# Routed attention and gated MLP on one core: the first two token tiles of the output layer also as a seven-product pair, with a rewritten order of work

## The chip, the cores and the metric

One Trainium2 chip, one of its cores. The metric is the device time of one execution in microseconds (us). The kernel before took 300.97 us (median of 3 runs, 300.54 to 301.33).

## What is computed

Four batches of eight heads attend over 768 tokens of 64 values. A query sees a key only if both are nearest to the same one of 16 centroids of their head. The heads' outputs side by side are the 512 features of 3072 tokens, which pass through a layer of 2048 gated units and an output layer.

```python
q_assign = argmax(einsum('bhsd,hcd->bhsc', q_n, c_n))      # k_assign likewise
mask = q_assign[:, :, :, None] == k_assign[:, :, None, :]
scores = where(mask, scale * q @ k.T, -1e9)
attn = exp(scores - max); attn = attn / (sum(attn) + 1e-9)
x = (attn @ v).transpose(0, 2, 1, 3).reshape(B * S, H * D)
h = x @ w_in;  g = h / (1 + exp(-h));  out = g @ w_out
```

## The kernel before

The order of all work is written by hand. `plan` (L722) is a list of short entries; the loop behind it reads them one after the other and `step` (L604) issues the instructions of each. Every engine runs its own instructions in the order of the list, and waits only for data and for buffers. An entry is an operation, a number, perhaps an engine (`A` ScalarE, `D` VectorE, `P` GpSimd) and perhaps a bank of PSUM (0 to 3). A bank is free again when its content has been read out. Two more pairs of banks hold scores.

The entries that the text below uses, with their functions:

- `r`, `hi`, `lo`, `ht`: load q and k of a head (SP's queue), split into a high and a low half-precision part, transpose by DMA into `ab` (SP's queue). `vl`, `v`: load and cast V.
- `L` or `l`, `ls`, `mx`, `ge`, `cm`, `ce`: routing. Logits on TensorE, sum, maximum and compare on VectorE, two transposes of the one-hot rows on TensorE (`cd_mm`, L216), their evacuation (`cd_ev`, L225, ScalarE or VectorE), which then goes by DMA into the rows of `ab` that add the mask to the scores.
- `qk` and `ex` (L315, L328): a unit is a head, a half of the queries and two key tiles: two score matmuls and one exponential. There are 192 units, and two score buffers, so qk of unit u+2 waits for ex of unit u. 48 units are a batch.
- `pv`, `nm`, `pt` or `xd`, `pe`: attention times V into a bank, normalisation on VectorE, transpose by TensorE or DMA into `xt`, evacuation.
- `e`, `t`, `g` (L388, L400, L404): four matmuls for a block of 128 hidden features and 384 tokens into a bank, tanh on ScalarE, gate on VectorE into `gt`; `e` 0 to 15 are the first half of batch 0, 16 to 31 the second.
- `b`, `bo` (L412, L419): a quarter of the plain output layer for one token tile, four matmuls of 512 columns; its evacuation on VectorE and store.
- `wc` (L434): combinations of quarters of `w_out` for the pairs, kept in `store`, or written over one quarter of it.
- `m`, `S`, `z`, `o` (class `Pair`, L445): the output layer for two token tiles by Strassen's scheme. Seven products of eight matmuls of 256 columns (`m`), four sums of gated tiles on VectorE (`S`), three intermediate evacuations on ScalarE (`z`), four outputs (`o`, one on ScalarE, three on VectorE). The number is ten times the pair's place in `duos` (L602) plus the step.
- `w`: weight loads through GpSimd's queue, each behind a small copy that reads the newest exponential's output; `w8` to `w11` are the four parts of `w_out`.

Before the change the tiles of a batch form the pairs (0, 1), (2, 5) and (3, 4), but in batch 0 tiles 0 and 1 are plain: `b0` to `b7`, `bo0`, `bo1`. The list puts them between units 42 and 48, where the first batch's second half is not yet gated.

Of the kernel before, what the change touches and what calls it, by code (L numbers as in the profile page):

```python
# [29 lines left out]
def kernel(  # L30
# [571 lines left out]
    duos = [Pair(b, x, y) for b in range(B) for x, y in ((0, 1), (2, 5), (3, 4)) if (b, x) != (0, 0)]  # L602

    def step(op, n, eng, banks):  # L604
# [133 lines left out]
        lo13 mx8 L10.2 ge8 cm8 mx10 ex44 b3 ex45 ce8.A wc1 ge10 bo0 pv6.1 nm6 qk46 l9.0 cm10 vl15 ht13 ls9 mx9 wc2 ge9
        qk47 hi12.A lo12 vl13 ht12 wc12 b4.3 ce10.A ex46 pt6.2 b5 cm9.0 ex47 hi14.A ce9.A pe6.A lo14 r16 pv7.1 nm7 b6
        L11.2 wc8 pt5.0 pe5.A pt7.1 pe7.A b7 mx11 ge11 cm11 v10.A v8.A ce11.A hi15.D qk48 e24.0 r17 ht14 bo1 lo15 ht15  # L740
        vl9 v11 vl14 vl16.P t24 g24 e21.3 t21 e18.2 qk49 g21 ex48 l13.1 ls13 mx13 e22.3 t18 g18 ex49 qk50 r18 l12.1
        ls12 mx12 v15.D ex50 e27.0 t27 g27 vl17 hi17.P t22 g22 hi16.P e20.2 t20 g20 qk51 e19.1 ge12 e16.0 qk52 e23.3
        ex51 qk53 t16 t19 g19 g16 ex52 t23 ex53 e29.2 t29 g23 cm12.1 ce12.D ge13 qk54 ex54 e26.0 g29 e30.3 t30 t26
        e25.1 t25 qk55 ex55 qk56 v13.D l15.2 g30 g26 ls15 g25 e17.3 t17 e28.0 lo16 od2 qk57 cm13.1 e31.2 g17 S3 ex56
        wc13 wc14 ce13.A qk58 r20 ht16 v9 pv8.3 nm8 ex57 qk59 ex58 qk60 t31 L14.1 ex59 ex60 m1.3 mx15 wc7 mx14 ge15
        g31 qk61 qk62 ge14 t28 g28 m7 wc15 S13 ex61 ex62 lo17 cm14 ce14.A wc9 hi18.P lo18 cm15.0 ce15.A m11.2 wc3 qk63
        qk64 v16 pv9.1 nm9 z0 v17 ht17 r19 S1 ex63 ex64 qk65 m2.0 vl21.P qk66 ex65 z10 S2 wc10 S4 S11 wc11 ex66 qk67
        ex67 m17 qk68 m6 pv10.1 ex68 z1 hi20.D qk69 ex69 qk70 ex70 m5 o0 qk71 ex71 l17.0 S12 m16 z2 nm10 z11 ls17
        hi19.D lo20 qk72 l16.1 qk73 ex72 ex73 ht18 l18.0 o3 ls18 mx17 od1 ge17 m15 qk74 qk75 ls16 mx18 mx16 lo19 m3
        ex74 qk76 m4 S14 xd9 xd8 ex75 qk77 z12 v14.A pv11.1 o13 ex76 r21 ge16 vl19 r22 hi22.P qk78 xd10 ht19 m14 nm11  # L750
        ex77 ex78 qk79 o1 ge18 pt11.1 o12 ex79 pe11.A m12.0 vl18.P o2 m13 qk80 o11 qk81 o10 pv12.0 ex80 qk82 ex81
        e34.2 v21.A nm12 ex82 qk83 ex83 e35.0 t35 lo22 qk84 e33.3 cs16 cs18 hi21.P cs17 r23 lo21 g35 pv13.1 qk85 t34
# [5 lines left out]
        e47.2 t47 g47 qk99 r25 m21.0 qk100 ex99 qk101 l22.1 ls22 mx22 m22.2 l23.3 z20 ex100 ex101 qk102 o20 ex102 ge22
        S21 ls23 qk103 pv16.2 cv19 ex103 qk104 e48.3 qk105 ex104 ex105 mx23 S22 m26 cs22 v22.D z21 t48 ge23 qk106
        qk107 ex106 ex107 nm16 S24 r24 cx21 v20 m25 z22 m27.1 cx22 cv20 qk108 v19 pv17.2 qk109 o23 hi24.D vl23.P cs23  # L760
        xd16 cx23 v23.D cv21 ex108 qk110 m23 cv22 ex109 g48 nm17 o21 m24 o22 ex110 qk111 lo24 ht24 e49.2 ex111 qk112
        e50.1 cv23 t49 vl25.P ex112 g49 qk113 xd17 e51.3 v24 t50 ex113 qk114 g50 e52.2 t51 pv18.0 ex114 g51 t52 e53.1
# [67 lines left out]
```

## Time and profile before

| what | us |
|---|---|
| median of the runs | 300.97 |
| the profiled execution | 301.45 |
| its span from first to last instruction | 299.7 |
| TensorE busy | 289.5 |
| ScalarE busy | 233.6 |
| VectorE busy | 222.1 |
| GpSimd busy | 72.6 |

In the lines of the profile PE is TensorE (PEld its weight loads), DVE VectorE, ACT ScalarE, POOL GpSimd, SP the engine that issues most DMAs. A line of a timeline gives the start, the time until the end, engine, line of the code, operation, output<-inputs, shapes and count, and in brackets how long the engine stood idle before it and what ended that. TensorE's matmuls overlap, so the time between two starts tells more than the time of one. A line of a stretch gives its ends, its length, and for PE, PEld, DVE, ACT and POOL the busy time with the number of instructions, then TensorE's granted clock, the DMA engines' share and GB/s. A line of a group gives count, total busy time and mean ns of one.

### The profile page before, as it was taken

To read this page: it belongs to the slowest core of one execution; us is meant where nothing else is said; L and a number is where in the kernel's file an instruction comes from. 1 tells how busy PE (TensorE), PEld (TensorE's weight loads), DVE (VectorE), ACT (ScalarE), POOL (GpSimd) and SP (SyncE) were. 2 spreads that over 40 slices of the span, in tenths; PEclk is the share of its full clock that TensorE was granted. 3 is DMA by queue.
4 is the path that set the end of the run, shared out by engine and by line. 5 is a ranking of instruction groups with operands and counts; after the bars stand their busy time and mean duration, and the time that the engine had idled before them with its cause. 6 is when DMAs were issued, how large, how long until landed. Compare 5 with 4: busy or idle time off the path is not lost.

```text
span 299.7 us, 8579 instructions
## 1 busy us (share of the span) xinstructions
PE 289.5 (97%) x3433; PEld 212.7 (71%) x3433; DVE 222.1 (74%) x482; ACT 233.6 (78%) x410; POOL 72.6 (24%) x125
## 2 busy tenths in 40 slices
PE   8899999999999999999989999999999999999994
PEld 3767666567568887667856887767867886776683
DVE  5898848789899895878657987788756733666763
ACT  5999899957888888998879876898669768965631
POOL 2655802000172027224354014220420000000000
PEclk9999999999999999999999999999999999999999
DMA  6999999999976979894598535968221102211103
GB/s 209 293 252 240 195 195 174 188 239 217 232 201 160 171 180 266 182 166 103 133 212 202 166 68 112 248 158 125 52 88 35 26 5 79 74 28 35 38 18 126
DMA packets 75368, 44.13 MB, mean 147 GB/s; under 512 B 54288, under 2 KB 71216, under 8 KB 75328
## 3 DMA queue, kind: packets, MB, share of 16 engines
q1 hardware_dynamic: 70560, 36.14, 51.2%
q0 software_dynamic: 4480, 7.15, 12.9%
q8 instruction: 27, 0.44, 0.7%
q10 hardware_dynamic: 288, 0.30, 0.3%
q14 instruction: 13, 0.11, 0.1%
HBM read 27.30 MB, written 6.29 MB: 112 GB/s over the span
## 4 chain that ended last, share of the span: by engine, by line
PE 74%; DMA 13%; ACT 4%; DVE 3%; issue 2%; SPq 1%; POOL 1%; ACTq 0%; DVEq 0%; POOLq 0%
PE ph L390 22%; PE xb L477 18%; PE pS L325 15%; PE pO L342 9%; DMA vn<-in_v_dram 6%; DMA ab<-hl 4%; PE yb L477 3%; PE psN L159 3%; ACT P L330 2%; PE po L417 2%; DMA ab<-cdt 1%; DMA ab<-cd 1%; DMA raw<-in_q_dram 1%; PE wb L477 1%; DVE hl L112 1%
## 5 line engine op out<-in xcount | busy, mean ns | idle before, releaser
L330 ACT ACTIVATE P<-pS 128x768 f16<-128x768 f32 x192 | 151.2, 816 | 21.6 <-PE pS L325 20.1
L390 PE MATMUL ph<-xt,win_s 128*128 128x384 f16 x512 | 96.4, 326 | 0.0
L405 DVE SCALAR_TENSOR_TENSOR gt<-tn,ph 128x384 f16<-128x384 f32 x128 | 68.0, 550 | 32.8 <-ACT tn L402 32.0
L325 PE MATMUL pS<-ab 128*128 128x384 f16 x384 | 87.1, 326 | 1.4 <-DMA ab<-cdt 0.8
L402 ACT ACTIVATE tn<-ph 128x384 f32<-128x384 f32 x128 | 60.8, 499 | 13.5 <-PE ph L390 10.2
L390 PEld LDWEIGHTS <-win_s 128*128 128x128 f16 x512 | 49.4, 98 | 30.8
L325 PEld LDWEIGHTS <-ab 128*128 128x128 f16 x384 | 34.3, 98 | 17.8 <-DMA ab<-cdt 1.1
L342 PEld LDWEIGHTS <-P 128*128 128x128 f16 x1152 | 39.8, 97 | 4.2 <-DVE cd L234 0.4
L342 PE MATMUL pO<-vt,P 128*128 128x65 f16 x1152 | 41.2, 193 | 0.0
L477 PEld LDWEIGHTS <-gt 128*128 128x128 f16 x352 | 33.9, 98 | 6.4 <-DVE xn L354 0.3
L112 DVE SCALAR_TENSOR_TENSOR hl<-raw,hl 128x768 f16<-128x768 f32 (+3 forms) x35 | 31.4, 901 | 0.6 <-ACT hl L103 0.3
L105 POOL TENSOR_SCALAR hl<-raw 128x768 f16<-128x768 f32 (+1 forms) x11 | 22.8, 2074 | 34.9 <-DMA raw<-in_k_dram 20.2
L477 PEld LDWEIGHTS <-s 128*128 128x128 f16 x264 | 25.5, 98 | 4.5
L159 PEld LDWEIGHTS <-ab 128*128 128x128 f16 x544 | 18.9, 97 | 6.3 <-DMA ab<-hl 2.1
L477 PE MATMUL xb<-wout_s,gt 128*128 128x256 f16 x176 | 22.7, 273 | 0.2 <-DVE xn L354 0.2
L499 ACT ACTIVATE ot<-xb 128x256 f32<-128x256 f32 x33 | 12.7, 386 | 12.3 <-PE xb L477 12.0
L159 PE MATMUL psN<-stk,ab 128*128 128x16 f16 (+1 forms) x544 | 20.1, 184 | 1.7 <-DMA ab<-hl 0.7
L477 PE MATMUL xb<-wc,s 128*128 128x256 f16 x160 | 20.7, 273 | 0.0
L354 DVE TENSOR_TENSOR xn<-pO,zr 128x384 f16<-128x384 f32 x32 | 17.8, 557 | 1.1
L199 POOL TENSOR_SCALAR od<-od 128x96 f16<-128x96 f16 x16 | 8.9, 559 | 39.3 <-DVE od L192 39.1
L212 POOL DMA_DIRECT2D ab<-cdt x16 | 8.8, 547 | 33.2 <-PE pS L325 11.9
L490 DVE TENSOR_TENSOR s<-gt 128x1024 f16<-128x1024 f16 x22 | 15.7, 715 | 1.3 <-PE xb L477 1.0
(93 smaller groups left out, 258.5 us busy)
## 6 DMA issues: line engine op xcount, KB each, us to landing
raw<-in_k_dram SPq DMA_DIRECT2D x31, 192.0 KB, 3.9
raw<-in_q_dram SPq DMA_DIRECT2D x24, 192.0 KB, 4.0
out_dram<-ot SPq DMA_DIRECT2D x18, 256.0 KB, 2.6
vn<-in_v_dram SPq DMA_DIRECT2D x21, 192.0 KB, 4.5
vn<-in_v_dram POOLq DMA_DIRECT2D x11, 192.0 KB, 3.6
win_s<-in_moe_w_in_dram POOLq DMA_DIRECT2D x8, 256.0 KB, 7.3
wout_s<-in_moe_w_out_dram POOLq DMA_DIRECT2D x4, 512.0 KB, 9.4
out_dram<-ot SPq DMA_DIRECT2D x12, 128.0 KB, 1.8
```

What stands on the lines that cost most here:

```text
L105: nc.gpsimd.tensor_scalar(out=o, in0=i, scalar1=QS, scalar2=None, op0=ALU.mult)
L112: nc.vector.scalar_tensor_tensor(out=hl[:, s, 1, :], in0=raws[job.name][:, s, :], scalar=QS, in1=hl[:, s, 0, :], op0=ALU.mult, op1=ALU.sub ...
L159: nc.tensor.matmul(L[:, n % 2, :, n // 2], ab[:, i, :], stk[:, job.groups[i // 3][0], x : x + w], start=(x == 0), stop=(x + w == 2 * HC),)
L325: nc.tensor.matmul(pS[:, e, 0:HALF], abs_[kj.name][:, kn, :], rhs, start=True, stop=True)
L330: nc.scalar.activation(out=P, in_=pst.pop(u)[:, :, 0:HALF], func=AF.Exp, bias=0.0, scale=ESC)
L342: nc.tensor.matmul(o[:, (2 * t + h) * VW : (2 * t + h + 1) * VW], Ps[i + h, c, j // 2][:, j % 2, ts(t, 128)], vtb[(i + h) % 13][:, j, 0:VW ...
L354: nc.vector.tensor_tensor(out=xn, in0=ov[:, :, 0:D], in1=zr.unsqueeze(2).to_broadcast([128, 2 * NM, D]), op=ALU.mult)
L390: nc.tensor.matmul(ph[:, 0:HALF], win_s[:, r, ts(fb, 128)], xts[b, c][:, r, :], start=(r == 0), stop=(r == NR - 1))
L402: nc.scalar.activation(out=tn, in_=phs[b, c, fb][:, 0:HALF], func=AF.Tanh, bias=0.0, scale=0.5)
L405: nc.vector.scalar_tensor_tensor(out=gt[:, fb, NM * c : NM * c + NM, :].rearrange("p t n -> p (t n)"), in0=tns.pop((b, c, fb)), scalar=1.0 ...
L477: nc.tensor.matmul(o, self.lhs(l, f), self.rhs(r, f), start=(f == 0 and opens), stop=(f == HB - 1), skip_group_check=True)
L490: nc.vector.tensor_tensor(out=o, in0=a, in1=b_, op=op)
```

## The change

The pair (0, 1) of batch 0 is made like the others, so `b` and `bo` are gone, and the list of entries is another from unit 30 to about unit 102 and from unit 119 to about unit 141; between and behind these only the numbers of the pairs differ, which are higher by one (`m21` was the first pair of batch 1, `m31` is). The diff, with the list cut to a few of its lines:

```diff
-    duos = [Pair(b, x, y) for b in range(B) for x, y in ((0, 1), (2, 5), (3, 4)) if (b, x) != (0, 0)]
+    duos = [Pair(b, x, y) for b in range(B) for x, y in ((0, 1), (2, 5), (3, 4))]
...
-        t7 ht11 wc6 r15 qk41 e9.0 g15 t12 ex41 qk42 t9 b0.3 qk43 g7 b1 ex42 wc0 qk44 g12 g9 hi13.D L8.1 ex43 b2 qk45
...
+        qk39 ex38 ex39 hi11.D e8.0 ht9 lo11 pe4.A t14 t8 qk40 e12.2 ex40 ht11 g14 L8.3 qk41 qk42 t12 g12 ex41 ex42 g8
+        mx8 ge8 e7.1 v11 qk43 e9.0 wc4 cm8 ce8.D v10 t7 g7 wc8 ex43 qk44 e10.1 qk45 t9 g9 wc1 hi13.A lo13 t10 S3 wc5
...
```

In the new list the 16 projections of the second half of batch 0 and the score units 42 to 58 come ahead of the products; the first product stands behind `e17` and `qk58`. `hi12` to `hi15`, `hi17` and `hi19` are on ScalarE, `hi16` and `hi18` on VectorE; of these the old list has `hi16`, `hi17` and `hi18` on GpSimd.

The first place is VectorE's queue around the routing of head 8, from the low part of another head (L112) ahead of it. The first `mxn` and `om` (`om_90`) are the maximum and the one-hot rows of head 8, `cd` its evacuated transposes, `gt` gates, `wc` combinations of output weights, `s` a sum of the pair. Before:

```order
L112 SCALAR_TENSOR_TENSOR hl<-raw,hl 128x12x64
L183 TENSOR_REDUCE mxn<-psN 128x12
L192 TENSOR_TENSOR om_90<-psN,mxn 128x192
L183 TENSOR_REDUCE mxn<-psN 128x12
L443 TENSOR_TENSOR wc<-wc,wout_s 128x512
L192 TENSOR_TENSOR om_91<-psN,mxn 128x192
L422 TENSOR_SCALAR ot<-po 128x512
```

and now:

```order
L112 SCALAR_TENSOR_TENSOR hl<-raw,hl 128x12x64
L405 SCALAR_TENSOR_TENSOR gt<-tn,ph 128x384 x3
L183 TENSOR_REDUCE mxn<-psN 128x12
L192 TENSOR_TENSOR om_90<-psN,mxn 128x192
L443 TENSOR_TENSOR wc<-wout_s 128x512
L234 TENSOR_SCALAR cd<-psN,kadd 96x256
L405 SCALAR_TENSOR_TENSOR gt<-tn,ph 128x384
L443 TENSOR_TENSOR wc<-wout_s 128x512
L405 SCALAR_TENSOR_TENSOR gt<-tn,ph 128x384
L443 TENSOR_TENSOR wc<-wc,wout_s 128x512
L112 SCALAR_TENSOR_TENSOR hl<-raw,hl 128x12x64
L490 TENSOR_TENSOR s_97<-gt 128x1024
```

The evacuation of head 8's transposes (`cd`) has come from ScalarE to VectorE, with gates `g7` and `g9`, weight combinations and the sum S3 behind it; the plain tile's output copy (`ot<-po`) is gone.

The second place is ScalarE's queue from exponential ex31 on (`P`; `tn` is a tanh, `xt` a copy of attention output, `cd` as above, `hl` the high part of a head). Before:

```order
L330 ACTIVATE P<-pS 128x768 x3
L402 ACTIVATE tn<-ph 128x384 x2
L330 ACTIVATE P<-pS 128x768
L402 ACTIVATE tn<-ph 128x384
L330 ACTIVATE P<-pS 128x768 x2
L402 ACTIVATE tn<-ph 128x384 x3
L330 ACTIVATE P<-pS 128x768
L402 ACTIVATE tn<-ph 128x384
L330 ACTIVATE P<-pS 128x768 x3
L402 ACTIVATE tn<-ph 128x384 x2
L330 ACTIVATE P<-pS 128x768
```

and now:

```order
L330 ACTIVATE P<-pS 128x768 x3
L402 ACTIVATE tn<-ph 128x384
L330 ACTIVATE P<-pS 128x768 x3
L402 ACTIVATE tn<-ph 128x384
L330 ACTIVATE P<-pS 128x768 x3
L372 ACTIVATE xt<-px 128x384
L402 ACTIVATE tn<-ph 128x384 x2
L330 ACTIVATE P<-pS 128x768
L402 ACTIVATE tn<-ph 128x384
L330 ACTIVATE P<-pS 128x768 x2
```

The old piece ends with ex41, the new one with ex41 and ex42; the new one has four tanh fewer in this piece (three fewer counted from ex28 on), and one copy `xt` more, which VectorE did before.

The third place is SP's queue behind the load of `vl10`; `raw` are loads of q and k, `vn` loads of V, `ab<-hl` the transposes by DMA. Before:

```order
L264 DMA vn<-in_v_dram 128x384
L92 DMA raw<-in_q_dram 128x384
L92 DMA raw<-in_k_dram 128x384
L264 DMA vn<-in_v_dram 128x384
L92 DMA raw<-in_q_dram 128x384
L92 DMA raw<-in_k_dram 128x384
L121 DMA_TRANSPOSE ab<-hl 128x12x128 x3
```

and now:

```order
L264 DMA vn<-in_v_dram 128x384
L121 DMA_TRANSPOSE ab<-hl 128x12x128
L92 DMA raw<-in_q_dram 128x384
L92 DMA raw<-in_k_dram 128x384
L92 DMA raw<-in_q_dram 128x384
L92 DMA raw<-in_k_dram 128x384
L264 DMA vn<-in_v_dram 128x384
L121 DMA_TRANSPOSE ab<-hl 128x12x128 x3
```

The transpose of head 8 goes out ahead of the loads instead of behind them.

More of the change, by code (lines that the diff above doesn't have):

```diff
@@ L738 @@
[L738 to L752, printed above, removed]
@@ L758 @@
[L758 to L762, printed above, removed]
@@ new lines @@
+        g46 qk96 ex96 qk97 t42 v21.D g47 g42 pv15.2 nm15 qk98 vl19.P ex97 ex98 mx21 vl24.P e43.1 t43 cv18 e45.3 t45
+        xd13 xd14 vl20 ge21 g43 g45 xd15 S33 qk99 cs21 m31.0 qk100 ex99 qk101 l22.1 ls22 mx22 m32.2 l23.3 z30 ex100
+        ex101 qk102 o30 ex102 ge22 S31 ls23 qk103 pv16.2 cv19 ex103 qk104 e48.3 qk105 ex104 ex105 mx23 S32 m36 cs22
+        v22.D z31 t48 ge23 qk106 qk107 ex106 ex107 nm16 S34 r24 cx21 v20 m35 z32 m37.1 cx22 cv20 qk108 v19 pv17.2
+        qk109 o33 hi24.D vl23.P cs23 xd16 cx23 v23.D cv21 ex108 qk110 m33 cv22 ex109 g48 nm17 o31 m34 o32 ex110 qk111
```

94 lines of the change are left out of this document (54 added, 40 removed).

## Prediction

> **What bounds the kernel now.** I read the first part of the page, then the same busy times cut into stretches, then TensorE's timeline row by row. The page:
>
> ```profile
> span 299.7 us, 8579 instructions
> PE 289.5 (97%) x3433; PEld 212.7 (71%) x3433; DVE 222.1 (74%) x482; ACT 233.6 (78%) x410; POOL 72.6 (24%) x125
> ```
>
> TensorE (PE) carries the span; no other engine comes near. But PE's ends are modelled, so I take its work from the distance between starts, which I call a step. The stretch in which the list of order differs most runs from the first pair of score matmuls that both lists place alike (qk30) to the point where the remaining order is alike again (qk102). PE's timeline there:
>
> ```profile
> 43.88 0.81 PE L325 MATMUL pS<-ab 128*128 128x384 f16 x4
> 44.53 1.26 PE L342 MATMUL pO<-vt,P 128*128 128x65 f16 x36
> 45.62 0.49 PE L325 MATMUL pS<-ab 128*128 128x384 f16 x2
> 45.95 0.81 PE L390 MATMUL ph<-xt,win_s 128*128 128x384 f16 x4
> 46.60 0.49 PE L325 MATMUL pS<-ab 128*128 128x384 f16 x2
> ...
> 56.96 1.03 PE L417 MATMUL po<-wout_s,gt 128*128 128x512 f16 x4
> 57.83 0.49 PE L325 MATMUL pS<-ab 128*128 128x384 f16 x2
> ...
> 60.25 0.77 PE L159 MATMUL psN<-stk,ab 128*128 128x16 f16 x24 [0.75 <-DMA ab<-hl]
> ...
> 62.05 0.76 PE L159 MATMUL psN<-stk,ab 128*128 128x16 f16 x24
> 62.66 0.29 PE L221 MATMUL psN<-ident,om 128*96 128x128 f16 x2
> 62.78 1.03 PE L417 MATMUL po<-wout_s,gt 128*128 128x512 f16 x4
> ...
> 139.28 0.51 PE L159 MATMUL psN<-stk,ab 128*128 128x32 f16 x12
> 139.63 0.81 PE L325 MATMUL pS<-ab 128*128 128x384 f16 x4
> ...
> 142.67 1.04 PE L477 MATMUL xb<-wc,s 128*128 128x256 f16 x8
> 143.54 0.81 PE L325 MATMUL pS<-ab 128*128 128x384 f16 x4
> ```
>
> qk30 starts at 43.88 and qk102 at 139.63, 95.75 us later. Steps: two score pairs 43.88 to 44.53, so 0.325 a pair; a `pv` of 36 matmuls 1.09; a projection `e` of four 0.65; a plain output quarter `b` of four 512-wide matmuls 0.87; a product `m` of eight 256-wide ones 0.87; routing logits 0.61 (`L`) or 0.35 (`l`); two one-hot transposes `cm` 0.12, and so 0.18 for the three of a `pt`. Between the two points the old list has 72 qk, 42 e, 12 pv, 16 m, 8 b, 4 L, 12 l, 8 cm, 5 pt: 23.4 + 27.3 + 13.1 + 13.9 + 7.0 + 2.4 + 4.2 + 1.0 + 0.9 = 93.2. So PE stands still for only 95.75 - 93.2 = **2.6 us** here, 0.75 of it in the row that waits for a transposed tile. That is all a better order could win.
>
> **The change, part by part.** *Arithmetic on PE.* Eight `b` (8 x 0.87 = 7.0) go, seven `m` (7 x 0.87 = 6.1) come: -0.87 us. Both are priced in this trace, as 4 x 512 and 8 x 256 columns with the same step, and all of it lies on PE.
>
> The Trainium skill ("TensorE: Matmul & The Clock Gate", Back-to-back issue gap) speaks against this saving: it gives a sustained pace of some 131 ns a matmul at 512 columns and 81 ns at 128, by which cutting the width saves little. By an estimate from that page, near 98 ns at 256, 32 x 0.131 = 4.2 us would go and 56 x 0.098 = 5.5 come, +1.3 us, and the time of the forecast below would be 304.3 us. The rows above disagree (0.87 for four of 512 and for eight of 256).
>
> *Arithmetic elsewhere.* On DVE four sums of 0.61 and three output adds come and two output copies go; on ACT four evacuations come. Stores keep their number and bytes. Beside what they lie:
>
> ```profile
> 84.40:139.63 55.23, 54.52 (x726) 41.87 (x725) 45.98 (x98) 48.59 (x83) 18.26 (x28) 1.00 0.84 177
> 162.30:193.00 30.70, 30.70 (x374) 24.24 (x373) 24.49 (x51) 23.83 (x42) 6.79 (x13) 1.00 0.61 151
> ```
>
> After 84.4 DVE is busy 45.98 of 55.23 us and ACT 48.59, so these additions find room there; without it they would cost at most some 2.5 us of DVE. They are counted below where they fall earlier. The second re-ordered stretch lies in the second row: PE has no gap, DVE and ACT are 80% busy, and the list holds the same PE instructions. I take 0 and keep +-0.4.
>
> *Order in the first stretch.* This decides. The new list runs the attention ahead and leaves output products for later: between qk30 and qk48 PE had 27.0 us of the steps above and now has 19.2. ACT and DVE have hardly less than before, so they pace PE there. On SP the transpose of head 8 is moved past two pairs of loads and a V load, on POOL three casts leave for ACT and DVE. What comes later by that is first read on ACT behind ex43, so I cost it at nothing; where that cover fails is the second rival. Four terms give when PE reaches the first product m1, which in the new list opens the bank that the gate g28 on DVE frees.
>
> (1) ACT up to exponential ex41:
>
> ```profile
> 42.07 0.82 ACT L330 ACTIVATE P<-pS 128x768 f16<-128x768 f32 x1
> ...
> 49.72 1.53 ACT L330 ACTIVATE P<-pS 128x768 f16<-128x768 f32 x2
> 51.12 1.28 ACT L402 ACTIVATE tn<-ph 128x384 f32<-128x384 f32 x3
> 52.23 0.88 ACT L330 ACTIVATE P<-pS 128x768 f16<-128x768 f32 x1
> ...
> 56.66 0.83 ACT L330 ACTIVATE P<-pS 128x768 f16<-128x768 f32 x1
> ```
>
> and, from the groups by line, the copy of transposed tiles that the new list puts on ACT here:
>
> ```profile
> L372 ACT ACTIVATE xt<-px 128x384 f16<-128x384 f16 x4 | 1.9, 488 | 1.7 <-PE px L363 1.7
> ```
>
> Steps: exponential 0.70 (two from 49.72 to 51.12), tanh 0.37 (three to 52.23). The old list does 13 exponentials and 13 tanh from ex28 (42.07) to the start of ex41 (56.66): 13.9 of 14.6 us, so it loses 0.7. The new one does 14, 10 and one 0.49 copy to the end of ex41: 14.0, with the same loss 56.7.
>
> (2) qk43 needs ex41's buffer. Behind it PE does one `e` and then cm8: 56.7 + 0.33 + 0.65 + the 0.29 of row 62.66 = 58.0. The evacuation of cm8 now stands on DVE:
>
> ```profile
> L234 DVE TENSOR_SCALAR cd<-psC,kadd 96x256 f16<-96x256 f32 x1 | 0.5, 473 | 0.0
> ```
>
> With 0.4 of its 0.47, DVE is free for the gate g7 at 58.4. This is the added wait; all of DVE's queue stands behind it, and PE's next `e` waits for g7's bank.
>
> (3) From g7 to g28 DVE has 55 operations. Their steps, from rows that follow each other closely:
>
> ```profile
> 41.84 1.02 DVE L405 SCALAR_TENSOR_TENSOR gt<-tn,ph 128x384 f16<-128x384 f32 x2 [1.79 <-ACT tn L402]
> ...
> 65.65 0.55 DVE L168 TENSOR_REDUCE L<-psN 128x192 f32<-128x384 f32 x1
> 66.23 0.49 DVE L183 TENSOR_REDUCE mxn<-L 128x12 f32<-128x192 f32 x1
> 66.64 0.41 DVE L443 TENSOR_TENSOR wc<-wout_s,wc 128x512 f16<-128x512 f16 x1
> 66.98 0.35 DVE L192 TENSOR_TENSOR om<-L,mxn 128x192 f16<-128x192 f32 x1
> 67.25 0.95 DVE L112 SCALAR_TENSOR_TENSOR hl<-raw,hl 128x768 f16<-128x768 f32 x1
> 68.11 0.42 DVE L443 TENSOR_TENSOR wc<-wout_s 128x512 f16<-128x512 f16 x1
> ...
> 69.32 0.19 DVE L352 RECIPROCAL zr<-pO 128x6 f32<-128x6 f32 x1
> ...
> 70.02 0.41 DVE L443 TENSOR_TENSOR wc<-wout_s 128x512 f16<-128x512 f16 x1
> ...
> 98.07 0.69 DVE L490 TENSOR_TENSOR s<-gt 128x1024 f16<-128x1024 f16 x1
> 98.68 0.42 DVE L443 TENSOR_TENSOR wc<-wout_s,wc 128x512 f16<-128x512 f16 x1
> ```
>
> Gate 0.46 (1.02 less the 0.56 of one); logit sum 0.58; maximum 0.41; weight combination 0.34; compare 0.27; low part `lo` 0.86; normalisation 0.70; Strassen sum 0.61. 18 x 0.46 + 11 x 0.34 + 5 x 0.86 + 2 x 0.61 + 6 x 0.41 + 6 x 0.27 + 2 x 0.70 + 4 x 0.58 + one cast at most 0.86 = 26.2. So m1 starts near 58.4 + 26.2 = **84.6**. PE's own steps from qk30 to m1 are 36.1 and would allow 80.0, so PE stands 4.6 us.
>
> (4) From m1 to qk102 PE has 23 m, 43 qk, 16 e, 8 pv, 8 l, a cm and a pt: 56.2 us. DVE and ACT have less than that here (the row 84.40:139.63), so I add no wait. qk102 starts at 84.6 + 56.2 = 140.8 against 139.63: **+1.2 us**, that is -0.9 of work and +2.0 of standing. From there on the PE order is that of before.
>
> The profiled execution took 301.45 us, 1.75 around its span of 299.7; that is 0.5 above the median of 300.97. Added to the median: **302.1 us**. Bounds of the unknown: term 1's loss between 0 and twice 0.7; term 3 between 24.9 (a twentieth less) and 27.5 (waits for tanh as in the row above, in part). So m1 lies between 82.6 and 86.6, and the time between 300.1 and 304.1; half of that to each side is this case's own range, 301.1 to 303.1.
>
> **Rivals.**
>
> *DVE is quicker, and the order wins.* In the stretch 44 to 95 POOL casts 128x768 tiles beside DVE, and the sums are slow there:
>
> ```profile
> L490 DVE TENSOR_TENSOR s<-gt 128x1024 f16<-128x1024 f16 x2 | 1.9, 962 | 0.0
> ```
>
> 962 ns, against 0.69 us in the row at 98.07. The new list moves three such casts off POOL, and if POOL is what slows DVE, all 55 operations gain. At 10% less, 23.6, and without ACT's loss, m1 comes at 81.3 and qk102 at 137.5, 298.8 us; at half of both, 83.0 and 139.2, 300.5; I put it between, at 299.6. It decides for faster from the point where DVE's stretch is under 24 us, that is m1 before 82.5. Against it: the steps I used are from moments without such a cast too.
>
> *DVE waits for weights.* Behind g7 stands a weight combination that needs the last quarter of `wout_s`:
>
> ```profile
> 46.39 0.75 POOL L529 DMA_DIRECT2D wout_s<-in_moe_w_out_dram  x1 [0.53 <-issue]
> DMA to landing us min/median/max: 6.9/9.4/11.1
> ```
>
> Issued at 46.39 it lands at 57.5 with the longest of these; DVE comes to it at 58.9 and the margin is 1.4 us. In the new order a transpose and a load of SP's queue go out ahead of it, on the same DMA engines. If it comes 2.5 us later, DVE stands 1.1, m1 moves as much, 303.2 us.
>
> *The change does not do what it says*: seven narrower products, with 56 weight loads for 32, take PE as long as eight plain quarters. Then the 0.87 is not saved, 303.0 us. For it speaks only that each product is one more switch of operand; the equal steps at 56.96 and 142.67 speak against it.
>
> **How the numbers follow.** A measurement of this kernel can tell 0.3%, 0.9 us, from no change: 300.1 to 301.9. Forecast 0.53: as 302.1 is just beyond the upper border and its range reaches below it, 0.33 slower and 0.20 same. Quicker DVE 0.28: 0.25 faster, 0.03 same. Late weights 0.17 and dear products 0.02: slower. So faster 0.25, same 0.23, slower 0.52. The range runs from 299.1, half-way into the first rival, to 303.9, past the second: some 0.1 is left out at either end.
>
> **What would show it.** Right: PE's row reaches the first `xb` at 84 to 85; in the rows of 50 to 85 PE has many idle entries after DVE's gates and ACT's exponentials in place of the one after the DMA; DVE's cast L234 on `psN` starts near 58 and DVE is over 90% busy from there to 84; `xb` keeps a step of 0.87 for eight; from m1 to the score pair of unit 102 it takes 56 us. Wrong: `xb` before 82.5 (DVE or ACT quicker than their old steps), DVE idle behind a DMA of `wout_s`, or a loss after 141, where I count none.

## The result, and the profile after

| | before | after |
|---|---|---|
| median of 20 runs each, us | 300.30 | 301.86 |
| lowest and highest | 298.35, 302.07 | 300.70, 304.75 |
| the profiled execution | 301.45 | 301.82 |
| its span | 299.7 | 300.0 |

The ratio is 1.0061, with a 95% interval of 1.0040 to 1.0082: the change makes the kernel slower by 0.6%, 1.6 us between the medians. The forecast was 302.1.

The first lines of the changed kernel's page say as little as before. PE is busy for all but 10 us:

```profile
span 300.0 us, 8619 instructions
PE 289.6 (97%) x3457; PEld 215.3 (72%) x3457; DVE 222.3 (74%) x488; ACT 235.3 (78%) x413; POOL 67.1 (22%) x121
```

PE's timeline tells it, with the same points as in the prediction. 44.55 is qk30, 60.24 is e10 behind the gate g7, 68.08 is qk48, 85.42 is the first product m1, and 141.81 is qk102:

```profile
44.55 0.81 PE L325 MATMUL pS<-ab 128*128 128x384 f16 x4
45.67 0.81 PE L390 MATMUL ph<-xt,win_s 128*128 128x384 f16 x4 [0.31 <-DVE gt L405]
...
50.99 0.48 PE L325 MATMUL pS<-ab 128*128 128x384 f16 x2 [0.22 <-ACT P L330]
...
55.32 0.81 PE L390 MATMUL ph<-xt,win_s 128*128 128x384 f16 x4 [0.30 <-ACT xt L372]
...
58.93 0.28 PE L221 MATMUL psN<-ident,om 128*96 128x128 f16 x2
...
60.24 0.81 PE L390 MATMUL ph<-xt,win_s 128*128 128x384 f16 x4 [0.71 <-DVE gt L405]
...
65.55 0.96 PE L342 MATMUL pO<-vt,P 128*128 128x65 f16 x26 [0.41 <-ACT P L330]
...
67.91 0.34 PE L363 MATMUL px<-ident,xn 128*128 128x128 f16 x3 [0.53 <-DVE xn L354]
68.08 0.49 PE L325 MATMUL pS<-ab 128*128 128x384 f16 x2
...
74.96 1.46 PE L390 MATMUL ph<-xt,win_s 128*128 128x384 f16 x8 [0.23 <-DVE L L168]
...
85.42 1.04 PE L477 MATMUL xb<-wout_s,gt 128*128 128x256 f16 x8
...
141.81 0.81 PE L325 MATMUL pS<-ab 128*128 128x384 f16 x4
```

The reader is to see many small waits, behind ACT and DVE in turn, where the old list had, up to qk48, one of 0.75 us behind a transpose. The same stretch as sums, from g7 to m1, from m1 to qk102, and units 119 to 141:

```profile
59.64:85.42 25.78, 23.88 (x313) 16.68 (x313) 25.54 (x59) 23.61 (x45) 1.75 (x3) 1.00 1.04 198
85.42:141.81 56.39, 56.39 (x727) 44.50 (x725) 44.85 (x96) 45.89 (x79) 12.75 (x23) 1.00 0.81 179
163.50:194.20 30.70, 30.70 (x374) 24.25 (x373) 24.09 (x50) 23.82 (x42) 8.03 (x13) 1.00 0.69 153
```

DVE is busy for 25.54 of 25.78 us ahead of m1, ACT for 23.61. Behind m1 PE has no gap, and in the second reordered stretch it has as little as before.

**The account.** I call *stand* what is left when the steps of the prediction are taken from the distance between two of PE's starts; it holds the time that PE waits, and also the time that it loses by working more slowly than those steps. The two traces give:

| stretch | before: distance, steps, stand | after | after less before |
|---|---|---|---|
| qk30 to qk102 | 95.75, 93.17, 2.58 | 97.26, 92.33, 4.93 | +1.51 |
| qk102 to qk118 | 20.33, 19.33, 1.00 | 19.35, 19.33, 0.01 | -0.98 |
| qk118 to qk191 | 104.02, 103.96, 0.06 | 104.02, 103.96, 0.06 | 0.00 |

So the change lost 1.51 us where the list was rewritten, -0.84 of work and +2.35 of standing, and 0.98 came back just behind it. There the kernel before waited ahead of qk111 for a head's transposed one-hot rows, which a DMA puts into `ab`. Its chain and its PE rows:

```profile
146.69 4.00 DMA ab<-cdt
```

```profile
148.89 1.04 PE L477 MATMUL wb<-wc,gt 128*128 128x256 f16 x8
...
150.73 0.50 PE L325 MATMUL pS<-ab 128*128 128x384 f16 x2 [0.81 <-DMA ab<-cdt]
```

and the same place after, where qk111 follows its product at once:

```profile
151.07 1.04 PE L477 MATMUL wb<-wc,gt 128*128 128x256 f16 x8
151.94 0.49 PE L325 MATMUL pS<-ab 128*128 128x384 f16 x2
```

In these two executions, then, the change cost +0.53 us. Beside it qk30 came 0.67 us later, although the list ahead of it differs only in its last entries (`e2`, `t2` and `ht8` where `t1` and `e5` stood); in the twelve traces of the new list it starts anywhere from 43.06 to 44.82. And the last store landed 0.9 sooner behind the last matmul: from the start of the last product to the end it is 4.96 and 4.88 us in the two traces of the old list (the second is of an experiment below) and 4.04 to 4.45 in all twelve of the new one, a gain that the prediction did not have and whose cause the traces do not show. The medians differ by 1.56. The profiled execution of before was one of its longer ones, 1.15 above its median, that of after lies at its median; the remaining 1.0 us has no place in this pair of traces. The other trace of the old list lies 0.85 above its median and has a stand of a microsecond behind qk102 too. An execution of the old list without that stand would be shorter by about as much, and the loss would then be the 1.51 of the first row; that this is the usual execution is not shown.

### The profile page after: what moved, and what is told of

The parts are those of the page before. It is cut to its first block, busy times and chain, and to the rows that moved or that the text cites. A ratio compares the mean times of both kernels' runs of the same rounds, so it can differ in the third digit from the quotient of the medians.

```text
span 300.0 us, 8619 instructions
## 1 busy us (share of the span) xinstructions
PE 289.6 (97%) x3457; PEld 215.3 (72%) x3457; DVE 222.3 (74%) x488; ACT 235.3 (78%) x413; POOL 67.1 (22%) x121
## 4 chain that ended last, share of the span: by engine, by line
PE 79%; DMA 7%; DVE 5%; ACT 5%; issue 2%; POOL 1%; SPq 0%; ACTq 0%; POOLq 0%
PE ph L390 24%; PE xb L477 20%; PE pS L325 17%; PE pO L342 9%; DMA vn<-in_v_dram 5%; PE yb L477 3%; PE psN L159 3%; ACT P L330 2%; DMA raw<-in_q_dram 1%; DMA ab<-cd 1%; PE wb L477 1%; DVE hl L112 1%; DVE gt L405 1%; ACT hl L103 1%; ACT ab L144 1%
## 5 line engine op out<-in xcount | busy, mean ns | idle before, releaser
L402 ACT ACTIVATE tn<-ph 128x384 f32<-128x384 f32 x128 | 61.6, 500 | 12.5 <-PE ph L390 9.6
L477 PEld LDWEIGHTS <-gt 128*128 128x128 f16 x384 | 37.1, 98 | 7.2
L112 DVE SCALAR_TENSOR_TENSOR hl<-raw,hl 128x768 f16<-128x768 f32 (+3 forms) x35 | 31.9, 913 | 0.7 <-ACT hl L103 0.5
L477 PEld LDWEIGHTS <-s 128*128 128x128 f16 x288 | 27.9, 98 | 5.1
L272 POOL CAST vt<-vn 128x384 f16<-128x384 f32 x19 | 12.4, 661 | 55.1 <-DMA vn<-in_v_dram 55.1
L477 PE MATMUL xb<-wout_s,gt 128*128 128x256 f16 x192 | 24.6, 273 | 0.0
L499 ACT ACTIVATE ot<-xb 128x256 f32<-128x256 f32 x36 | 13.8, 384 | 11.5 <-PE xb L477 11.1
L477 PE MATMUL xb<-wc,s 128*128 128x256 f16 x176 | 22.8, 273 | 0.0
L105 POOL TENSOR_SCALAR hl<-raw 128x768 f16<-128x768 f32 (+1 forms) x8 | 16.3, 2034 | 12.9 <-ACT P L330 7.0
L508 DVE SCALAR_TENSOR_TENSOR ot<-xb,ot 128x256 f32<-128x256 f32 x20 | 8.5, 423 | 13.8 <-ACT ot L499 5.5
```

Of the source, the lines that this page charges most:

```text
L105: nc.gpsimd.tensor_scalar(out=o, in0=i, scalar1=QS, scalar2=None, op0=ALU.mult)
L112: nc.vector.scalar_tensor_tensor(out=hl[:, s, 1, :], in0=raws[job.name][:, s, :], scalar=QS, in1=hl[:, s, 0, :], op0=ALU.mult, op1=ALU.sub ...
L402: nc.scalar.activation(out=tn, in_=phs[b, c, fb][:, 0:HALF], func=AF.Tanh, bias=0.0, scale=0.5)
L477: nc.tensor.matmul(o, self.lhs(l, f), self.rhs(r, f), start=(f == 0 and opens), stop=(f == HB - 1), skip_group_check=True)
L499: nc.scalar.activation(out=o, in_=self.xb[:, 0:DH], func=AF.Copy, bias=0.0, scale=0.5)
```

## The experiments

Each kernel was timed beside the kernel before on the same chip. The stands are worked out from each kernel's one profiled execution, as above. It was the shortest of the kernel's runs in e1_dve_order, e2_wc_on_pool and e4_gate_first, and the longest in e5_norms_first, e8_more_dve and e13_head13_early. The experiments go by these full names, or in short as run e1, run e2 and so on; `e10` or `e12` without the word run are projections, as in the list.

| kernel | ratio to before | 95% | PE's stand qk30 to e12, to e10, to qk48, to m1, m1 to qk102 | qk30 to m1 |
|---|---|---|---|---|
| changed kernel | 1.0061 | 1.0040 to 1.0082 | 1.59, 0.93, 1.79, 0.50, 0.12 | 40.88 |
| e1_dve_order | 1.0278 | 1.0245 to 1.0312 | 1.59, 0.93, 1.27, 1.79, 6.14 | 41.65 |
| e2_wc_on_pool | 1.0111 | 1.0082 to 1.0141 | 1.59, 0.93, 1.57, 2.18, 0.11 | 42.34 |
| e3_plain_in_new_order | 1.0109 | 1.0074 to 1.0145 | 6.32 in all to the first quarter | 42.39 |
| e4_gate_first | 1.0033 | 1.0003 to 1.0063 | 1.59, 0.38, 2.17, 0.59, 0.11 | 40.80 |
| e5_norms_first | 1.0073 | 1.0039 to 1.0108 | 1.59, 1.90, 4.06, 1.17, 0.11 | 44.78 |
| e7_four_moves | 1.0055 | 1.0024 to 1.0087 | 1.12, 0.47, 1.36, 3.04, 0.11 | 42.05 |
| e8_more_dve | 1.0113 | 1.0067 to 1.0159 | 1.59, 0.93, 1.78, 2.59, 0.11 | 42.96 |
| e9_weights_wait_less | 1.0079 | 1.0049 to 1.0109 | 1.59, 0.93, 1.47, 1.31, 0.11 | 41.36 |
| e10_less_in_the_way | 1.0085 | 1.0050 to 1.0121 | 1.12, 0.47, 4.21, 1.41, 0.12 | 43.27 |
| e12_after_late_load | 1.0074 | 1.0050 to 1.0099 | 1.59, 0.94, 1.79, 1.23, 0.11 | 41.60 |
| e13_head13_early | 1.0055 | 1.0035 to 1.0075 | 1.12, 3.19, 2.30, 1.40, 0.11 | 44.08 |
| e11_before_early_load (before's list) | 1.0017 | 0.9988 to 1.0046 | | |

In runs e5, e10 and e13 not all of the stand is waiting: some 1.5 to 1.7 us of it is work at half the granted clock, as shown below for run e5.

The theory at the start was the prediction's: DVE's queue from g7 to g28 paces PE up to m1. Rivals: some other engine, or the landings of DMAs, hold m1 as well.

### Less work on DVE ahead of m1

Eleven operations are taken from DVE's queue ahead of g28 and done behind it; the orders of PE and ACT stay. (`hi16` and `hi18` come later too, with their low parts and transposes.)

```diff
-... S3 wc5 wc2 ... wc9 ... wc6 ... wc3 ... S1 ... wc13 ... wc7 ... wc10 ... hi18.D ... g28 ...
+... S3 ... g28 ... g17 S1 wc1 wc5 wc9 wc13 S2 ... wc3 wc7 wc11 wc15 ... S4 ... wc14 wc2 wc6 wc10 hi18.D lo18 ht18
```

> Same instructions as the changed kernel, and the same order on PE and ACT; on DVE nine weight combinations (9 x 0.34), the sum S1 (0.60) and one cast (0.46) stand behind the gate g28 instead of ahead of it, so that DVE has 4.1 us less between g7 and g28. Theory (DVE's queue paces PE up to the first product): the first product starts 2 to 2.6 us earlier than the 85.4 of the changed kernel, at 82.8 to 83.4, because PE's own steps from cm8 (58.9) take 23.3 us and become the limit; the time falls by about 2 us to 299.8, ratio to the kernel before 0.998. Rival A (ACT, or the round trip through four banks, paces): the first product stays at 85.4, ratio 1.006. Rival B (DVE only owes the work): the first product is earlier, but PE stands for the sums behind it and the time falls by less than 0.5 us.

The stretch from g7 to m1, to be read against the row 59.64:85.42:

```profile
58.15:84.70 26.55, 24.07 (x313) 16.37 (x313) 22.36 (x47) 23.67 (x45) 1.92 (x3) 1.00 1.02 212
```

DVE has 47 operations here instead of 59 and is busy 3.2 us less, but the stretch takes 26.55 us instead of 25.78. PE's rows say what took DVE's place, and what the moved work does later:

```profile
69.05 0.52 PE L159 MATMUL psN<-stk,ab 128*128 128x32 f16 x12 [1.23 <-DMA ab<-hl]
...
95.78 1.03 PE L477 MATMUL xb<-wout_s,gt 128*128 128x256 f16 x8 [1.09 <-DVE cd L234]
...
102.29 1.03 PE L477 MATMUL xb<-wout_s,s 128*128 128x256 f16 x8 [3.61 <-DVE ot L508]
```

The logits of head 13 (l13, at 69.05) wait for its transpose by DMA, a wait that the changed kernel's trace does not have. With what comes of it in PE's starts it is 1.40 us; by an estimate from these rows, m1 would without it have come 40.25 us behind qk30, 0.6 sooner than in the changed kernel, for 3.2 us less of DVE. And between m1 and qk102, where the prediction found room on DVE, PE stands 6.14 us instead of 0.12. The room is not where the work came to stand; just behind m1 the changed kernel's DVE has none, 9.73 of 10.00:

```profile
85.00:95.00 10.00, 10.00 (x139) 8.50 (x138) 9.73 (x22) 8.39 (x15) 1.78 (x3) 1.00 0.85 165
```

That DVE alone paces is refuted; m1 was to come 2 to 2.6 us earlier.

### The same work on GpSimd

```diff
-... t7 g7 wc8 ... wc1 ... wc5 wc2 ... wc9 ... wc6 ... wc3 ... wc12 ... wc13 ... wc7 ... wc10 ...
+... t7 g7 wc8.P ... wc1.P ... wc5.P wc2.P ... wc9.P ... wc6.P ... wc3.P ... wc12.P ... wc13.P ... wc7.P ... wc10.P ...
```

> The changed kernel with the eleven weight combinations between g7 and g28 on POOL, which is idle there, so DVE loses 11 x 0.34 = 3.7 us. Theory (DVE's queue paces, and POOL does not hurt it): first product at 82.5 to 83.4, time down by about 2 us, ratio 0.998 to the kernel before. Rival (POOL and DVE hinder each other, as the 962 ns sums beside POOL casts suggested): each DVE operation beside a combination is longer, the first product comes at 85 or later, ratio 1.006 or more.

Ratio 1.0111, as the rival had it. DVE and POOL side by side:

```profile
59.89 1.28 DVE L112 SCALAR_TENSOR_TENSOR hl<-raw,hl 128x768 f16<-128x768 f32 x1 [0.17 <-ACT hl L103]
61.10 1.64 DVE L490 TENSOR_TENSOR s<-gt 128x1024 f16<-128x1024 f16 x1
62.15 1.61 POOL L443 TENSOR_TENSOR wc<-wout_s,wc 128x512 f16<-128x512 f16 x1
62.66 0.54 DVE L405 SCALAR_TENSOR_TENSOR gt<-tn,ph 128x384 f16<-128x384 f32 x1
```

A combination that takes DVE 0.42 takes POOL 1.15 to 1.9 us, and beside it DVE's sum takes 1.64 instead of the 0.68 it has in the changed kernel and `lo` 1.28 instead of 0.95, while the gate, which reads PSUM, keeps its 0.54. The Trainium skill ("SBUF — State Buffer", SBUF: two separate sides) says that a GpSimd operation that reads SBUF and a VectorE operation with two SBUF inputs lock each other out for a whole instruction; the extra 0.96 us of the sum and 0.33 of `lo`, each less than the 1.15 of the shortest POOL operation, can be such waits, though no row shows the lock itself. So the first rival's mechanism exists. But taking three casts off GpSimd did not bring its gain: that rival needed DVE's stretch under 24 us, and the changed kernel's is 25.78. And l13 waits for its DMA here too, 0.54 us.

### The plain tiles in the new order

Tiles 0 and 1 plain again, at the places of the pair's products; the sums, `z` and `o` of the pair go, and four combinations that overwrite `wout_s` come behind the last quarter.

```diff
-... m1.1 qk59 m7 ... S2 ... z0 m6 ... S4 ... m2.2 ... z1 ... m5 ... z2 o3 ... m3 ... o0 m4 ... o1 ... o2 ...
+... b0.1 b1 qk59 b2 ... b3 bo0 ... b4.2 ... b5 ... b6 ... b7 bo1 wc3 wc7 wc11 wc15 ...
```

> The new order with tiles 0 and 1 plain again: eight quarters at the places of the seven products, the four sums of that pair gone, the in-place weight combinations behind the last quarter. It takes the pair alone away. PE gets 0.87 us more work; DVE gets two sums (1.2) and two combinations (0.7) less between g7 and g28. Theory (DVE paces): the first quarter starts 1.9 us earlier than the first product did, at 83.5, and the whole is about 1 us shorter than the changed kernel, ratio to the kernel before 1.002 to 1.004: the pair costs more than it saves in this order. Rival A (the pair simply saves its PE work): 0.9 us longer than the changed kernel, ratio 1.009. Rival B (products are dear): more than 1.5 us shorter, and the product rows show a step over 0.87.

Ratio 1.0109 against 1.0061, some 1.4 us slower than with the pair, with intervals that overlap. That is nearest to rival A; the theory had the kernel about 1 us shorter. A quarter keeps its step, two of them from 85.95 to the next at 87.68:

```profile
85.95 1.89 PE L417 MATMUL po<-wout_s,gt 128*128 128x512 f16 x8
```

So the order without the pair is slower than the kernel before by about 1.1%, clear of the noise: the loss is the order's. The pair wins some of it back, about the 0.87 us that the prediction gave it as far as these intervals can tell. By the estimate that the prediction made from the Trainium skill ("TensorE: Matmul & The Clock Gate", Back-to-back issue gap) this kernel would have been the quicker one. The runs disagree: four matmuls of 512 columns take 0.87 us, 218 ns each, and eight of 256 take 0.87, 109 each, in every trace here.

### More work on DVE

```diff
-... t27 g27 wc13 ... g18 ex50 ... g16 hi17.A ... g25 qk51 ... g29 e26.1
+... t27 g27 wc12 wc13 ... g18 wc12 ex50 ... g16 wc12 hi17.A ... g25 wc12 qk51 ... g29 wc12 e26.1
```

> The changed kernel with one weight combination (wc12) done five times more on VectorE, between g27 and g29, 5 x 0.34 = 1.7 us. Theory of the prediction (VectorE paces until g28): m1 1.7 us later counted from qk30, 42.6. Local theory (from qk48 on PE runs at its own steps with little slack on VectorE): new stands of at most 1.7 less the slack, and the slack is what this shows; if VectorE had 0.5 to 1 us of it, m1 comes 0.7 to 1.2 us later.

m1 comes 42.96 us behind qk30 instead of 40.88, and DVE is again full:

```profile
59.90:87.80 27.90, 24.26 (x314) 16.69 (x314) 27.63 (x64) 24.35 (x45) 1.29 (x3) 1.00 0.96 184
```

Five operations more, 2.1 us more of DVE, and 2.1 us more to m1. The five account for some 1.8: their steps are 0.34 and once 0.45, also between gates. The rest is a `lo` with a step of 1.18 instead of 0.86 (at 77.48, where POOL casts a V). The prediction's theory foretold 1.7 us; the local one, with its slack of 0.5 to 1 us, foretold less. With the first experiment it makes one picture: DVE has no slack, so an addition costs in full, but taking from it gained nothing, since another wait, in that trace the one for head 13's transpose, stands close behind.

### Clearing single stands

Head 8's evacuation behind the gate:

```diff
-... cm8 ce8.D v10 t7 g7 wc8 ...
+... cm8 v10 t7 g7 ce8.D wc8 ...
```

> The changed kernel with one entry moved: head 8's evacuation ce8 stands behind the gate g7 on VectorE instead of ahead of it. Local theory (VectorE stops PE only at single places: 0.87 us before e10 through ce8 ahead of g7, 1.33 us before the two transposes pt6 and pt7, 0.40 before e21): the stand before e10 falls from 0.87 to about 0.45 us, the others stay, m1 comes 0.3 to 0.5 us earlier counted from qk30 (40.4 instead of 40.87). Theory of the prediction (VectorE's whole queue from g7 to g28 paces PE): the order of two of its entries changes nothing in its sum, m1 stays at 40.9 from qk30.

PE's row for e10:

```profile
58.78 0.81 PE L390 MATMUL ph<-xt,win_s 128*128 128x384 f16 x4 [0.15 <-DVE gt L405]
```

The stand falls by 0.55 where the local theory had some 0.4, and 0.47 of it is back by m1: 40.80 from qk30, where the theory of the prediction had 40.9 and the local one 40.4. The ratio, 1.0033, is the lowest of the new order, but its interval, 1.0003 to 1.0063, holds the changed kernel's 1.0061.

Normalisations ahead of four combinations:

```diff
-... S3 wc5 wc2 e15.2 ... wc9 qk46 ... wc6 nm7 ... ge11 wc12 ... S12 qk66 ...
+... S3 e15.2 ... qk46 ... nm7 ... ge11 wc5 wc9 wc12 ... S12 wc2 wc6 qk66 ...
```

> The changed kernel with four weight combinations moved on VectorE: wc5 and wc9 from ahead of nm6 to behind ge11, wc2 and wc6 to behind S12, past g28. Local theory: the stands before pt6 and pt7 fall from 1.33 us together to about 0.6, since both normalisations come up to 1.4 us earlier; what then comes earlier may meet head 13's transpose by DMA, which in the runs with less VectorE work landed near 69; m1 0.3 to 0.7 us earlier counted from qk30. Theory of the prediction: 0.7 us of VectorE work leave the queue ahead of g28, so m1 comes 0.7 us earlier, wherever the stands are.

Ratio 1.0073. The profiled execution took 304.89 us, the longest of this kernel's 12, and shows something else. DVE's row of wc8, PE's row behind it, and the landings of the four loads of `wout_s`, here and then in the changed kernel:

```profile
63.12 0.43 DVE L443 TENSOR_TENSOR wc<-wout_s 128x512 f16<-128x512 f16 x1 [2.85 <-DMA wout_s<-in_moe_w_out_dram]
```

```profile
64.06 0.33 PE L363 MATMUL px<-ident,xn 128*128 128x128 f16 x3 [1.95 <-DVE gt L405]
```

```profile
DMA to landing us min/median/max: 7.6/12.5/16.8
```

```profile
DMA to landing us min/median/max: 6.1/9.6/10.8
```

This is the second rival of the prediction, DVE waiting for weights, in an execution of a kernel that has wc8 where the change put it: the longest of the four loads took 10.8 us in one execution and 16.8 in another.

Behind that stand PE worked more slowly. Its two next `pv`, 72 matmuls, and then TensorE's granted clock from the page, one digit for each 7.6 us, where 9 is 90% or more:

```profile
65.57 3.82 PE L342 MATMUL pO<-vt,P 128*128 128x65 f16 x72
69.22 0.33 PE L363 MATMUL px<-ident,xn 128*128 128x128 f16 x3
```

```profile
PEclk9999999989999999999999999999999999999999
```

The `pv` take 3.65 us instead of 2 x 1.09, and cut finer the granted clock is 0.50 from 65.5 to 68.5. So 1.5 us of this kernel's stand is no wait. The same follows the stand of 1.73 us in the trace of run e10 (the same two `pv` take 3.72) and that of 2.59 in run e13's: some 3.4 us at a granted clock of 0.50 each time. Over the whole execution the clock is then 0.994. Of the twelve executions of run e5's kernel, and of the twelve of run e13's, only the traced one has that, so these two traces show exceptions and not what sets the medians. And the four runs of the changed kernel above 303 us have 0.999 or 1.000: whatever made them long, it was not this.

All of it and a little more, in run e7: both moves, the copy pe4 on DVE, head 13's transpose ahead of head 14's loads on SP.

```diff
-... pt4.2 qk38 wc0 ... lo11 pe4.A t14 ... L10.3 r14 ht13 r15 ...
+... pt4.2 pe4.D qk38 wc0 ... lo11 t14 ... L10.3 ht13 r14 r15 ...
```

> The changed kernel with both of these moves, with the copy pe4 on VectorE instead of ScalarE, and with head 13's transpose ahead of head 14's loads on SP. Local theory: stands before e12 (0.47), e10 (0.87), pt6 and pt7 (1.33) fall by 1.5 to 2 us together and head 13's transpose is no wait, m1 at 39.0 to 39.4 from qk30, qk102 that much earlier; the wait of 0.97 us before qk111 that the kernel before had may come back in part; time 0.3 to 0.6% under the changed kernel, that is 300 to 301 us, even with the kernel before. Theory of the prediction: only the 0.7 us that leave the queue count, m1 at 40.2, time 0.2% under the changed kernel.

Ratio 1.0055, where the local theory had the time of the kernel before. The stands up to qk48 fall by 1.4 us, nearly as that theory said, and those from qk48 to m1 grow by 2.5:

```profile
68.21 0.52 PE L159 MATMUL psN<-stk,ab 128*128 128x32 f16 x12 [0.87 <-DMA ab<-hl]
...
71.25 2.25 PE L390 MATMUL ph<-xt,win_s 128*128 128x384 f16 x12 [0.97 <-ACT cd L232]
```

```profile
69.62 0.84 ACT L103 ACTIVATE hl<-raw 128x768 f16<-128x768 f32 x1 [2.63 <-DMA raw<-in_q_dram]
```

l13 still waits for its transpose, and ACT stands 2.63 us for head 14's load, which went out behind that transpose now, with the evacuation behind it that PE's next projection needs. The gain was given back, most of it to DMA.

### DMA in the way

wc8 and wc9, which read the last quarter of `wout_s`, some 7 us later:

```diff
-... g7 wc8 ex43 ... pe5.A wc9 qk46 ... nm7 pt7.1 ...
+... g7 ex43 ... pe5.A qk46 ... nm7 wc8 wc9 pt7.1 ...
```

> The changed kernel with wc8 and wc9, the first combinations that read the last quarter of the output weights, moved on VectorE from ahead of nm6 to behind nm7, some 7 us later. Theory of the late weights (in one profiled execution VectorE stood 2.85 us at wc8 for that load, which landed at 62.8 instead of 57.6): the longest runs, up to 304.75 us in 20 runs of the changed kernel, go, none is over 303.5; the shortest stay near 300.7. The stands before pt6 and pt7 fall from 1.33 to about 0.6 us. Median 301.2, ratio to before 1.003. Rival (the spread comes from elsewhere and the sum of VectorE's work decides): spread and median as the changed kernel's, 1.006.

Ratio 1.0079, runs from 301.53 to 303.00. None is as long as the changed kernel's longest, though six runs are few to say so. The median is no lower, where 301.2 was foretold: the stands before pt6 and pt7 are 1.20 us together instead of 1.34, and the two combinations now make the logit sum late for which L11 waits:

```profile
68.92 0.75 PE L159 MATMUL psN<-stk,ab 128*128 128x16 f16 x24 [0.59 <-DVE L L168]
```

That load itself later, behind ex35 instead of ex30, with wc8 and wc9 as above, g7 ahead of ce8, pe4 on DVE, wc2 and wc6 behind S12:

```diff
-... qk31 g3 r12 lo9 w11 r13 ... ex35 qk37 ...
+... qk31 g3 r12 lo9 r13 ... ex35 w11 qk37 ...
```

> The changed kernel with that move, and also: the last quarter of the output weights issued behind exponential ex35 instead of ex30, g7 ahead of ce8, pe4 on VectorE, wc2 and wc6 behind S12. Theory (once single stands on VectorE are cleared the landings of the transposes by DMA set the floor, as in the runs with stands before l13 and L10, and a load of 512 KB less ahead of them lowers it): stands before e12, e10, pt6 and pt7 fall by 1.5 to 2 us together and none comes before L10 or l13, m1 at 39.2 to 39.6 counted from qk30, time 300.2 us, even with before. Rival (VectorE's sum up to g28 still holds m1): 0.7 us of work fewer, m1 at 40.2.

Ratio 1.0085, and the opposite of what was foretold: PE waits for head 10's transpose, and then has the half clock.

```profile
63.05 0.77 PE L159 MATMUL psN<-stk,ab 128*128 128x16 f16 x24 [1.73 <-DMA ab<-hl]
```

Head 13 early, as the last attempt at a better version:

```diff
-... ex40 ht11 g14 L8.3 ... cm8 ce8.D v10 t7 g7 wc8 ... g9 wc1 hi13.A lo13 ... r14 ht13 r15 ... ge11 wc12 ...
+... ex40 ht11 g14 hi13.D L8.3 ... cm8 v10 t7 g7 ce8.D ... g9 lo13 ht13 wc1 ... r14 r15 ... ge11 wc8 wc9 wc12 ...
```

(with pe4 on DVE, and wc2 and wc6 behind S12.)

> The changed kernel with g7 ahead of ce8, pe4 on VectorE, hi13 on VectorE in its idle stretch behind g14, lo13 right behind g9, head 13's transpose right behind that on SP ahead of head 14's loads, wc8 and wc9 behind ge11, wc2 and wc6 behind S12. Theory (the stretch up to unit 48 is held by several limits of nearly equal height, single stands on VectorE and the landing of head 13's transpose the highest two): stands before e12, e10, pt6 and pt7 fall by 1.5 to 2 us together, none before l13, perhaps 0.5 before L10 for head 10's transpose; m1 at 39.0 to 39.6 counted from qk30, time 299.5 to 300.5 us, ratio to before 0.997 to 1.001. Rival (DMA as a whole holds the stretch: whatever is cleared, some transpose or load lands later and takes it): stands move to L10, l13 or a cast behind a load and sum up as in the changed kernel, m1 at 40.9 or later, ratio 1.005 to 1.008.

Ratio 1.0055, as the rival had it. Its profiled execution, 303.98 us, was again the longest of 12. The chain of waits there, and PE's row for it:

```profile
45.87 10.76 DMA raw<-in_q_dram
56.62 1.39 issue
58.01 0.56 DVE hl L107
```

```profile
59.55 0.81 PE L390 MATMUL ph<-xt,win_s 128*128 128x384 f16 x4 [2.59 <-DVE gt L405]
```

DVE's queue stands behind `hi13` for a load that was out for 10.76 us (and for 1.39 more for which the profile gives no reason), and PE behind DVE. The stretch 44 to 60 in the changed kernel, in e5_norms_first and here (the last two columns are the DMA engines' share and GB/s):

```profile
44.00:60.00 16.00, 14.70 (x168) 9.34 (x166) 11.77 (x24) 15.45 (x28) 2.90 (x6) 1.00 1.22 233
```

```profile
44.00:60.00 16.00, 14.00 (x163) 8.85 (x161) 11.16 (x23) 14.52 (x26) 2.82 (x6) 1.00 1.32 160
```

```profile
44.00:60.00 16.00, 12.88 (x157) 8.42 (x155) 10.64 (x22) 13.67 (x24) 3.25 (x5) 1.00 1.27 186
```

The engines of DMA are about as full in all three, and moved 233, 160 and 186 GB/s. No version of the new order came out below the changed kernel beyond the intervals, and none beats the kernel before.

### The microsecond behind qk102

The first thought was SP's queue: the change has head 25's loads at unit 88 instead of 99, where two pairs of loads stood ahead of the transposes that feed qk111. The kernel before with `r25` at unit 91, and the changed kernel with `r25` back:

```diff
-... g39 qk91 ge20 ... qk99 r25 m21.0 ...
+... g39 qk91 r25 ge20 ... qk99 m21.0 ...
```

> The kernel before with one entry moved: head 25's loads r25 from unit 99 to unit 91, where the change has them at unit 88. Theory (the change won 0.97 us before qk111 because SP no longer issues two pairs of loads between 138 and 142 ahead of the transposes that feed qk111): the stand of 0.97 us before qk111 falls to under 0.3, nothing else moves, time 0.7 to 1.0 us under before, ratio 0.997. Rival (the change won it because PE came 2 us later while SP's chain did not): the stand stays at 0.9, ratio 1.000.

```diff
-... vl22 r25 m23 ... S33 qk99 cs21 ...
+... vl22 m23 ... S33 qk99 r25 cs21 ...
```

> The changed kernel with r25 put back to unit 99, behind qk99. Theory of the load: the stand before qk111 comes back, 0.5 to 1.0 us, time as much longer, ratio to before 1.008 to 1.0095. Rival (PE's later arrival): no stand there, time as the changed kernel's, 1.006.

The first has no stand before qk111, but one of 1.09 us at e48 and qk105, behind DMAs of an attention output and of one-hot rows, and a ratio of 1.0017:

```profile
143.25 0.32 PE L390 MATMUL ph<-xt,win_s 128*128 128x384 f16 x1 [0.93 <-DMA xt<-xn]
```

The second has 0.13 us from qk102 to the end, and 1.0074. So the load alone is not the cause: neither kernel fits the theory, and run e12 came out as its rival, PE's later arrival, had foretold. What remains: both profiled executions of the old list stand a microsecond behind qk102 for a DMA, and of the twelve of the new list two stand there for one, and for less (run e3 0.26 us, run e9 0.53). Which of its earlier entries, or PE's later arrival, makes the difference stays open.

Run e12 is of use for the main question too. Up to unit 87 it is the changed kernel, entry for entry, and its l13 waits for head 13's transpose:

```profile
69.11 0.52 PE L159 MATMUL psN<-stk,ab 128*128 128x32 f16 x12 [0.63 <-DMA ab<-hl]
```

The same order meets DMA in one execution and misses it in the next.

## Why the prediction was right, point by point

The time was right (302.1 against 301.86), and so was the sign, but that the time is met so closely is partly luck. The forecast added 1.2 us to a median of three runs, 300.97; over twenty runs that kernel has 300.30, and the change added 1.56. One number was 0.7 too high, the other 0.4 too low. Of its steps:

- *Arithmetic, -0.87.* Right: PE's steps from qk30 to qk102 fall by 0.84, products take 0.87 for eight matmuls, and the experiment with plain tiles agrees that the pair saves.
- *Step 1, ACT up to ex41.* Near. ex41 and ex42 start at 57.09, so ex41 ends at 57.8 with its step of 0.70, where 56.7 was said; 0.67 of this is the later qk30, some 0.4 is ACT's.
- *Step 2, g7 behind ce8.* Right in kind, and shown by moving ce8: the stand ahead of e10 falls from 0.87 to 0.32. g7 starts 0.6 later than said, beside the 0.67:

```profile
57.09 1.51 ACT L330 ACTIVATE P<-pS 128x768 f16<-128x768 f32 x2
...
59.24 0.48 DVE L234 TENSOR_SCALAR cd<-psN,kadd 96x256 f16<-96x256 f32 x1
59.64 0.54 DVE L405 SCALAR_TENSOR_TENSOR gt<-tn,ph 128x384 f16<-128x384 f32 x1
...
84.79 0.56 DVE L405 SCALAR_TENSOR_TENSOR gt<-tn,ph 128x384 f16<-128x384 f32 x1
```

- *Step 3, 26.2 us of DVE from g7 to m1.* The number is near, 25.78, and m1 came 40.88 us behind qk30 where 40.7 was said; here too two errors cancel, a stretch 0.4 shorter than said behind a g7 that is 0.6 late. The reason given for it is half of the truth. DVE is full there, and what is added to it is paid in full. But it does not pace alone: with 3.2 us less on DVE m1 came no earlier, and with single stands cleared PE met the transpose of head 13, the loads, or ACT. Which wait ends the stretch in an untraced execution is not shown. A queue that is full is a lower bound; that the time equals the bound does not make it the cause.
- *Step 4, 56.2 us from m1 to qk102 without a wait.* Right: 56.39, with a stand of 0.12, and the same 56.4 in ten of the eleven traced executions of the new list that have the pair. The room on DVE that it named is real (44.85 of 56.39), but lies behind 95; the first experiment shows what happens to work put in front of it.
- *Nothing behind qk102.* This failed, in its words "From there on the PE order is that of before". The order was, but PE in the old kernel stood 0.98 us in there, for a DMA, and the sum carried all of the +1.2 past it. An upstream loss of 1.51 left 0.53 in these two traces. The second reordered stretch is 0, as said.
- *The rivals.* Quicker DVE did not happen, and the experiment on GpSimd shows why it was a rival: POOL's work does slow DVE's SBUF operations. DVE's wait for weights did not happen in the changed kernel's profiled execution, but in one of a near relative of it, 2.85 us long. The changed kernel's runs reach 304.75 us, but none above 303 has the lower clock of that one, so that such a wait makes its spread is not shown. Dearer products are refuted.

What stays open: how much of the 1.56 us between the medians comes from the late landings that single executions show, since only one execution of either kernel has a trace, and how often the old list has its stand behind qk102.

## What to carry to other kernels

Where several engines are nearly full at once (here VectorE for 25.54, ScalarE for 23.61 and TensorE for 23.88 of 25.78 us) and DMA landings lie close, adding to the fullest cost in full and relieving it gained nothing; look for what stands second before counting a gain. A delay is not carried to the end unchanged: go through the waits of the old trace behind it, and take off what they absorb. A load's landing time in one trace is one draw: wc8, some 2 us behind the landing of its weights in one execution, waited 2.85 us in another. And read the clock of a trace before its waits: a late matmul is not always a waiting one.
